# Prefix sums of 14 routing batches as 64-row matmuls around the swap of the row groups

## The chip, the cores and the metric

The kernel runs on one core of one Trainium2 chip. The metric is the device time of one execution in microseconds (us). Engines are named as in the profile: PE (TensorE matmuls), PEld (TensorE weight loads), DVE (VectorE), ACT (ScalarE), POOL (GpSimd), SP (SyncE, which here only issues DMAs).

## The reference

Two parts follow one another: a gated attention unit without softmax, and a mixture of experts with one expert per token beside a dense branch.

```python
# attention: u, v (8, 2816, 256), z (8, 2816, 64)
scores = (1 / S) * (z @ z.T)                 # per batch element
out = np.maximum(scores, 0) ** 2 @ v
x = (u * out).reshape(22528, 256)
# mixture of experts: 8 experts, D 256, F 512
y_dense = relu(x @ w1_dense) @ w2_dense
logits = x @ w_gate
e = argmax(logits); gate = softmax(logits)[e]
y = y_dense + gate * (relu(x @ w1[e]) @ w2[e])
```

For the second part tokens are sorted by expert. Each token's place among the tokens of its expert is a prefix sum over tokens of the one-hot choice, and that sum is what the change touches.

## The kernel before, in words

**Two stages.** Tokens are handled in blocks of 128 (176 blocks, 22 for each of the 8 batch elements). In the attention stage scores, squares and products with `v` are computed, and, block by block, each token's expert and place, after which its row is scattered into the DRAM buffer `xs`, sorted by expert. In the expert stage (`slot`) tiles of sorted rows are fetched, run through the dense branch and one expert, and scattered to the output. The change lies in the attention stage.

**The attention stage.** `scores` (L391) multiplies 64-row pieces of `zT` (the depth of z is 64). `zT` holds z twice, in partitions 0 to 63 and 64 to 127, so that two matmuls run beside each other, one in each half of TensorE's rows (a *row group*), each with its own PSUM bank. `relu` (L413) lets ACT or DVE scale and clamp the result into `r`, and ACT, DVE or at the beginning POOL square it into a key tile `A`. `av` (L578) multiplies two blocks of `A` with `v` into one PSUM pair `o`: 88 matmuls of 64 rows and 256 columns, in two passes. In the first pass row group 0 writes bank 0 and row group 1 bank 1; in the second they change banks (`j = p ^ h`). Each bank collects the sum over both halves of the rows in this way, with no addition afterwards.

**The swap.** Between the passes stands `swap_rows` (L556). It sets something between the last writes of the one row group and the first writes of the other into the same bank: a `touch` (L549, a 64-row matmul of 8 columns into a spare PSUM pair `x`) and two score steps, the first into a pair of its own and the second into `x`; where there are no scores to do, a second touch takes their place.

**PSUM.** There are four pairs of banks (`NS = 4`). `take_pair` and `give_pair` hand them out; `o`, scores, touches, logits and prefix sums all live in one. `keep` holds pairs back near the end of a pass, so that the swap and the next `av` call find one.

**Order of the work.** Engine queues run in program order, and the program order comes from a planner inside the kernel. It carries a planned time `now`, planned times at which ACT, DVE and POOL are free, a list `todo` of offered operations with ready times and ranks, and planned release times of the PSUM pairs. `run(t)` issues what is due until `t`. `fill` (L508), called after every second step of `av`, either starts a due entry of `jobs` when a pair is free, or a score step. `tick` runs after every half `av` call, starts what is listed in `later`, and offers one scatter.

**Routing.** Blocks are routed in 18 batches (`sizes`: 14 of 11 blocks, then 8, 6, 4, 4). `routing(q)` (L1089) puts `first` on `jobs`: it takes a pair, computes `logits` (L652, 2 full-row matmuls of 8 columns for each block) and offers `route_a`, which turns them into the one-hot matrix `oh` (tokens in partitions, experts x blocks along the row). `middle` returns the pair and puts `second` on `jobs`, due 2.5 planned us later. `second` takes a pair, calls `route_pre` (L686) and chains the three DVE steps of `route_b` (L696) behind it. `route_pre` computes, per expert and block, the number of tokens (`ones` times `oh`) and minus the tokens at or after each token (`ntri` times `oh`) into `pre`. `route_b` adds the running base and reads out the places. `last` returns the pair and puts the batch's blocks on the list of `waiting` scatters.

**Scatters and the ring of rows.** `gate_x` (L627), one DVE operation per `av` call, multiplies `o` with `u` into `pays`, a ring of 22 blocks. A scatter (`scatter`, L743: a DVE cast `pi` and a POOL indirect DMA) must have read a block of `pays` before the gate of 22 blocks later overwrites it. Loads of `v`, `z` and the weights are issued by POOL into the same software queue as the scatters.

Of the kernel before, what the change touches and what calls it, by code (L numbers as in the profile page):

```python
# [15 lines left out]
P = 128  # L16
# [3 lines left out]
def kernel(  # L20
# [12 lines left out]
    nc = tc.nc  # L33
    B, S, D = u.shape
    dq = z.shape[2]
    E = moe_w_gate.shape[1]
# [5 lines left out]
    G = 11  # L42
# [3 lines left out]
    nQ = len(sizes)  # L46
# [37 lines left out]
    def banks(x, name, shape=(P, 2, 4 * P), dt=F32):  # L84

        return ps.tile(list(shape), dt, name=name, tag=f"b{x}")
# [7 lines left out]
    ones = const.tile([P, P], BF, name="ones")  # L94
    ntri = const.tile([P, P], BF, name="ntri")
# [39 lines left out]
    now = [0.0]  # L135
# [5 lines left out]
    z_of, zn_of, zT_of, v_of, ut_of, xT_of, lg_of, rs = {}, {}, {}, {}, {}, {}, {}, {}  # L141
# [145 lines left out]
    pairs = [(0.0, x) for x in range(NS - 2)]  # L287
# [42 lines left out]
    def run(until):  # L330
        while True:
            pick = best()
            if pick is None or pick[0][0] > until:
                return
            give(pick)

    def until(cond):

        while cond() is None:
            pick = best()  # L340
            assert pick is not None
            now[0] = max(now[0], pick[0][0])
            give(pick)
        now[0] = max(now[0], cond())
        run(now[0])
# [14 lines left out]
    left, far, key_at = {}, {}, {}  # L360
# [23 lines left out]
    def take_pair():  # L384
        return pairs.pop(0)[1]

    def give_pair(t, x):
        pairs.append((t, x))
        pairs.sort()
# [116 lines left out]
    jobs = []  # L506
# [13 lines left out]
    def ahead(n):  # L520

        for m in range(n, min(n + 3, len(groups))):
            if left[m]:
                if m == n + 2 and (turning and turning[0][0] <= m - 3 or read_at.get(m - 3, 0.0) > now[0]):
                    return None
                return m if groups[m][0] in z_there else None
# [22 lines left out]
    def touch(x):  # L549

        d = banks(x, "d", (P, 8))
        nc.tensor.matmul(out=d[:], lhsT=ones[0:dq, :], rhs=ones[0:dq, 0:8],
                         start=True, stop=True)
        pe(0.03)

    def swap_rows(n):  # L556

        keep[0] = 0
        if ahead(n) is None:
            until(lambda: pairs[0][0] if pairs else None)  # L560
            x = take_pair()
            touch(x)
            touch(x)
            give_pair(now[0] + 0.1, x)
            return
        until(lambda: pairs[1][0] if len(pairs) > 1 else None)
        x = take_pair()
        touch(x)
        m = ahead(n)
        scores(m, left[m].pop(0))  # L570
        m = ahead(n)
        if m is None:
            touch(x)
            give_pair(now[0] + 0.1, x)
        else:
            scores(m, left[m].pop(0), x)
# [67 lines left out]
    bank_of = {}  # L644

    def small(q, name, shape):
        if q < nQ - 2:
            return banks(bank_of[q], name, shape)
        tag = "y" if q == nQ - 2 else "s"
        return late[tag].tile(list(shape), F32, name=name, tag=tag)  # L650
# [34 lines left out]

    def route_pre(q):  # L686
        oh, ex = rs[q]
        pre = small(q, "pre", (P, 2, E * G))
        pre = [pre[:, i, :E * sizes[q]].rearrange("p (e t) -> p e t", e=E) for i in range(2)]
        nc.tensor.matmul(out=pre[0], lhsT=ones[:], rhs=oh, start=True, stop=True)  # L690
        nc.tensor.matmul(out=pre[1], lhsT=ntri[:], rhs=oh, start=True, stop=True)
        rs[q] = (oh, ex, pre)

    first_of = [0]

    def route_b(q):  # L696

        n = sizes[q]
        oh, ex, pre = rs[q]
        inc = vec("inc", E, n)  # L700

        def one():
            se = vec("se", n)
            nc.vector.tensor_reduce(out=se, in_=ex, axis=AX.X, op=ALU.add)
            o = starts[q] % (2 * G)
            rows = pays[:, o:o + n, :]
            nc.vector.reciprocal(rows.bitcast(F32)[:, :, P], se)
            nc.vector.tensor_copy(rows.bitcast(I32)[:, :, P + 1], tok[:, starts[q]:starts[q + 1]])
            assert q != Q1 or made_first[0]
            if first_of[0] != n:  # L710

                first_of[0] = n
                nc.vector.memset(smask[:, :E * n], 1.0)
                nc.vector.memset(smask[:, :E * n].rearrange("p (e t) -> p e t", e=E)[:, :, 0], 0.0)

        def two():
            tb = vec("tb", E, n)
            nc.vector.tensor_copy(tb, pre[0])
            nc.vector.tensor_add(tb[:, :, 0], tb[:, :, 0], base[:])
            nc.vector.tensor_tensor_scan(  # L720
                out=inc.rearrange("p e t -> p (e t)"), data0=smask[:, :E * n],
                data1=tb.rearrange("p e t -> p (e t)"),
                initial=0.0, op0=ALU.mult, op1=ALU.add)
            nc.vector.tensor_copy(base[:], inc[:, :, n - 1])

        def three():
            nc.vector.tensor_add(inc, inc, pre[1])
            nc.vector.tensor_mul(inc, inc, oh)
            pos = vec("pos", n, bufs=5)
            nc.vector.tensor_reduce(out=pos, in_=inc.rearrange("p e t -> p t e"),  # L730
                                    axis=AX.X, op=ALU.add)
            rs[q] = pos

        return [one, two, three]
# [312 lines left out]
    for b in range(B):  # L1047
        t = b * nK
# [30 lines left out]
    def chain(t, fns, then):  # L1079

        def done(t):
            if fns[1:]:
                chain(t, fns[1:], then)
            else:
                then(t)

        offer(t, 0.5, {"dve": (0.8, lambda eng: fns[0]())}, done)

    def routing(q):  # L1089
        def first():  # L1090
            bank_of[q] = take_pair()
            logits(q)
            now[0] += 0.6
            offer(now[0] + 0.2, 0, {"dve": (1.3, lambda eng: route_a(q))}, middle)

        def middle(t):
            give_pair(t, bank_of[q])
            jobs.append((t + 2.5, second))

        def second():  # L1100
            bank_of[q] = take_pair()
            route_pre(q)
            now[0] += 0.25
            chain(now[0] + 0.2, route_b(q), last)

        def last(t):
            give_pair(t, bank_of[q])
            routed.append(q)
            waiting.extend(range(starts[q], starts[q + 1]))

        jobs.append((now[0], first))
# [12 lines left out]
    for q in range(nQ - 2):  # L1124
        t = starts[q + 1] - 1 + LAG
# [26 lines left out]
    for n, (b, i0, w) in enumerate(groups):  # L1152
        for i in range(i0, i0 + w, 2):
# [3 lines left out]
            av(n, i, lambda: tick(g))  # L1157
            tick(g + 1)
    run(9e9)
    while jobs:  # L1160
        jobs.pop(0)[1]()
        run(9e9)
# [3 lines left out]
    for s in range(NT - MAYBE + 2):  # L1166
# [4 lines left out]
        if s % 3 == 1 and waiting:  # L1171
# [5 lines left out]
    n = nc.values_load(used[0:1, 0:1], min_val=0, max_val=NH,  # L1177
                       skip_runtime_bounds_check_because="made by the table")
# [34 lines left out]
```

## Time and profile before

| | |
|---|---|
| median of 3 runs | 913.24 us (909.78 to 918.02) |
| profiled execution | 911.23 us, span 909.5 us, granted clock 0.998 |
| PE busy | 866.3 us, 95% of the span, 12194 matmuls |
| ACT, DVE, POOL busy | 701.5 us (77%), 667.9 us (73%), 475.8 us (52%) |
| o matmuls in the attention stage | 459.9 us busy, 7184 from `A` and 560 from `wall` |
| full-row prefix matmuls | 18 + 18, from 70.2 to 568.0 us |
| DMA | mean 150 GB/s |

A row of a timeline gives the start and the time from the first start to the last end of a merged run of instructions, then line, operation, output<-input, shape and count; in brackets stands the idle time before it and what ended that. A shape `64*128 64x256` is a weight tile of 64 rows and 128 columns and a moving operand of 64 rows and 256 columns. Matmuls overlap, so the spacing of starts counts, not the duration of one.

### The profile page before, as it was taken

The page shows a single profiled execution, that of the slowest core. Times are in us where ns is not written, and L with a number is a line of the kernel's source. Part 1 is how long each engine was busy: PE and PEld are TensorE (multiplying, and loading weights), DVE is VectorE, ACT ScalarE, POOL GpSimd, SP SyncE. Part 2 cuts the span into 40 slices and gives each one's busy share as a digit, 9 for nine tenths or more (in the row PEclk, how much of TensorE's full clock was granted, in tenths as well). Part 3 has the DMA queues.
Part 4 walks back from the last instruction along what each step waited for, and adds up shares of the span by engine and source line. Part 5 has one row for each costly group of instructions (what it writes and reads, how often), then busy time and mean ns, then how long its engine had stood idle before and what let it go on. Part 6 is the DMA issues. An engine that isn't in the chain of part 4 may idle for free. (4 is left out here: it accounts for less than half of the span.)

```text
span 909.5 us, 30158 instructions
## 1 busy us (share of the span) xinstructions
PE 866.3 (95%) x12194; PEld 757.0 (83%) x12194; DVE 667.9 (73%) x1277; ACT 701.5 (77%) x872; POOL 475.8 (52%) x518
## 2 busy tenths in 40 slices
PE   8999999999999999999999999888989999999996
PEld 5898798898898898898888887777878887888885
DVE  7998897998898898889889975555634444456664
ACT  7988797898898888889879973657767676777664
POOL 8202343343443343353344343777878887877664
PEclk9999999999999999999999999999999999999999
DMA  9999999999999989999989966555444444444433
GB/s 178 156 198 156 183 187 172 206 180 184 201 185 175 207 177 184 202 180 183 207 167 163 158 138 104 116 121 109 113 106 112 113 105 109 112 103 100 96 91 80
DMA packets 289294, 136.80 MB, mean 150 GB/s; under 512 B 258686, under 2 KB 266110, under 8 KB 289152
## 3 DMA queue, kind: packets, MB, share of 16 engines
q1 hardware_dynamic: 263552, 79.40, 52.0%
q0 software_dynamic: 25600, 55.44, 26.1%
q8 instruction: 96, 1.57, 0.7%
q14 instruction: 46, 0.38, 0.1%
HBM read 61.54 MB, written 37.16 MB: 109 GB/s over the span
## 5 line engine op out<-in xcount | busy, mean ns | idle before, releaser
L604 PE MATMUL o<-vb,A 64*128 64x256 bf16 x7184 | 459.9, 269 | 2.5 <-ACT A L434 1.5
L604 PEld LDWEIGHTS <-A 64*128 64x128 bf16 x7184 | 379.9, 94 | 42.7 <-ACT A L434 3.5
L750 POOL DMA_INDIRECT xs<-pays,pi x176 | 189.5, 1076 | 278.3 <-DVE pi L748 228.2
L421 ACT ACTIVATE r<-s 128x1024 f32<-128x1024 f32 (+1 forms) x252 | 248.1, 1011 | 43.3 <-PE s L406 40.4
L965 ACT ACTIVATE ring<-h_ps 128x1024 bf16<-128x1024 f32 x180 | 185.5, 1032 | 89.8 <-PE h_ps L962 46.2
L434 ACT ACTIVATE A<-r 128x1024 bf16<-128x1024 f32 (+1 forms) x238 | 241.9, 1046 | 7.9 <-DMA wall<-A 3.3
L986 DVE SCALAR_TENSOR_TENSOR ring<-yy,me,ring 128x256 f32<-128x256 f32 x180 | 86.5, 482 | 152.4 <-ACT ring L985 83.7
L436 DVE TENSOR_TENSOR A<-r 128x1024 bf16<-128x1024 f32 x151 | 183.1, 1223 | 3.5 <-ACT A L434 1.4
L423 DVE TENSOR_SCALAR r<-s 128x1024 f32<-128x1024 f32 (+1 forms) x145 | 176.1, 1221 | 8.1 <-PE s L406 5.5
L988 POOL DMA_INDIRECT out_dram<-ring,me x140 | 148.9, 1064 | 63.1 <-DVE ring L986 29.4
L970 PEld LDWEIGHTS <-ring 128*128 128x128 bf16 x1440 | 139.9, 98 | 41.2 <-issue 25.5
L406 PE MATMUL s<-zT 64*128 64x512 bf16 (+1 forms) x874 | 146.5, 357 | 4.0 <-DVE pays L631 1.3
L970 PE MATMUL yy<-w2d,ring 128*128 128x256 bf16 x720 | 107.9, 272 | 19.5 <-DVE ring L986 16.6
L970 PE MATMUL yy<-ring 128*128 128x256 bf16 x720 | 108.0, 273 | 0.0
L962 PE MATMUL h_ps<-ring,w1d 128*128 128x256 bf16 x720 | 94.1, 273 | 3.1 <-DVE pays L631 1.6
L962 PE MATMUL h_ps<-ring 128*128 128x256 bf16 (+1 forms) x880 | 94.8, 253 | 0.9 <-issue 0.7
L985 ACT COPY ring<-yy 128x256 f32<-128x256 f32 x180 | 68.0, 378 | 34.0 <-PE yy L970 17.2
L950 DVE COPY ring<-wall 128x2048 bf16 x110 | 82.0, 761 | 12.7 <-issue 7.0
L631 DVE TENSOR_TENSOR pays<-o,ut 128x512 bf16<-128x512 f32 x88 | 60.4, 686 | 32.4 <-PE o L604 19.9
L962 PEld LDWEIGHTS <-ring 128*128 128x128 bf16 x880 | 73.4, 98 | 10.6 <-issue 1.9
L962 PEld LDWEIGHTS <-w1d 128*128 128x128 bf16 x720 | 70.0, 98 | 12.0 <-issue 3.5
L406 PEld LDWEIGHTS <-zT 64*128 64x128 bf16 x874 | 55.1, 94 | 21.3 <-issue 9.6
(122 smaller groups left out, 437.1 us busy)
## 6 DMA issues: line engine op xcount, KB each, us to landing
ut<-in_u_dram SPq DMA_DIRECT2D x88, 256.0 KB
vb<-in_v_dram POOLq DMA_DIRECT2D x14, 704.0 KB
wall<-in_moe_w_dram POOLq DMA_DIRECT2D x16, 256.0 KB
xs<-pays,pi POOLq DMA_INDIRECT x176
zr<-in_z_dram POOLq DMA_DIRECT2D x7, 352.0 KB
out_dram<-ring,me POOLq DMA_INDIRECT x140
ring<-xs SPq DMA_TRANSPOSE x114
xT<-pays SPq DMA_TRANSPOSE x88
```

What stands on the lines that cost most here:

```text
L406: nc.tensor.matmul(out=s[:, h, y * c:(y + 1) * c], lhsT=zT[r, k + h, :], rhs=zT[r, i0:i0 + w, :], start=True, stop=True)
L421: nc.scalar.activation(r[:, :, :c], s[:, :, :c], AF.Relu, scale=1.0 / S)
L423: nc.vector.tensor_scalar(out=r[:, :, :c], in0=s[:, :, :c], scalar1=1.0 / S, scalar2=0.0, op0=ALU.mult, op1=ALU.max)
L434: nc.scalar.activation(a, r, AF.Square)
L436: (nc.gpsimd if eng == "pool" else nc.vector).tensor_mul(a, r, r)
L604: nc.tensor.matmul(out=o[:, j, 0:D], lhsT=block(n, k, i + j - i0)[r], rhs=v_of[b][r, k, :], start=(p == 0 and x == 0), stop=(p == 1 and x ...
L750: ins = nc.gpsimd.indirect_dma_start(out=xs, out_offset=bass.IndirectOffsetOnAxis(ap=pi[:], axis=0), in_=pays[:, g % (2 * G), 0:ROW].bitca ...
L962: nc.tensor.matmul(out=h_ps[:, f, hs, :], lhsT=w1(c, f), rhs=xT[:, hs, c, :], start=(c == 0), stop=(c == 1))
L965: nc.scalar.activation(h, h_ps[:].rearrange("p f h t -> p f (h t)"), AF.Relu)
L970: nc.tensor.matmul(out=y[:, k, :], lhsT=h[:, f, j * P:(j + 1) * P], rhs=w2(f), start=(f == 0), stop=(f == 3))
L986: nc.vector.scalar_tensor_tensor(out=ys, in0=y[:, 1, :], scalar=me[:, j, 0:1], in1=yd, op0=ALU.mult, op1=ALU.add)
L988: ins = nc.gpsimd.indirect_dma_start(out=out, out_offset=bass.IndirectOffsetOnAxis(ap=ids[j], axis=0), in_=ys, in_offset=None, bounds_chec ...
```

## The change

For the first 14 routing batches `second` no longer goes to `jobs` but to a list of its own, `at_swap`. The next `swap_rows` that finds an entry due takes it. It runs the prefix matmuls as 64-row pieces: two before the touch (row group 0 with `ones` into bank 0, row group 1 with `ntri` into bank 1), and two after it (row group 0 with `ntri` into bank 1, row group 1 with `ones` into bank 0), which add up with the first two in the two banks. Between them stand the touch and one score step into the touched pair (or a second touch); a usual swap has two score steps there. The last four batches keep the full-row form.

```diff
+    at_swap = []
+
     def swap_rows(n):
 
         keep[0] = 0
+        if at_swap and at_swap[0][0] <= now[0]:
+            fn = at_swap.pop(0)[1]
+            until(lambda: pairs[1][0] if len(pairs) > 1 else None)
+            fn(0)
+            x = take_pair()
+            touch(x)
+            m = ahead(n)
+            if m is None:
+                touch(x)
+                give_pair(now[0] + 0.1, x)
+            else:
+                scores(m, left[m].pop(0), x)
+            fn(1)
+            return
...
     def route_pre(q):
         oh, ex = rs[q]
-        pre = small(q, "pre", (P, 2, E * G))
+        pre = banks(bank_of[q], "pre") if q < nQ - 4 else small(q, "pre", (P, 2, E * G))
         pre = [pre[:, i, :E * sizes[q]].rearrange("p (e t) -> p e t", e=E) for i in range(2)]
-        nc.tensor.matmul(out=pre[0], lhsT=ones[:], rhs=oh, start=True, stop=True)
-        nc.tensor.matmul(out=pre[1], lhsT=ntri[:], rhs=oh, start=True, stop=True)
         rs[q] = (oh, ex, pre)
+        if q < nQ - 4:
+            pre_part(q, 0)
+        else:
+            nc.tensor.matmul(out=pre[0], lhsT=ones[:], rhs=oh, start=True, stop=True)
+            nc.tensor.matmul(out=pre[1], lhsT=ntri[:], rhs=oh, start=True, stop=True)
+
+    def pre_part(q, p):
+
+        oh, _, pre = rs[q]
+        for h in range(2):
+            r = slice(h * dq, (h + 1) * dq)
+            j = p ^ h
+            nc.tensor.matmul(out=pre[j], lhsT=(ones, ntri)[j][r, :], rhs=oh[r],
+                             start=(p == 0), stop=(p == 1))
+        now[0] += 0.04
...
         def middle(t):
             give_pair(t, bank_of[q])
-            jobs.append((t + 2.5, second))
-
-        def second():
-            bank_of[q] = take_pair()
-            route_pre(q)
-            now[0] += 0.25
-            chain(now[0] + 0.2, route_b(q), last)
+            if q < nQ - 4:
+                at_swap.append((t + 2.5, second))
+            else:
+                jobs.append((t + 2.5, lambda: second(0)))
+
+        def second(p):
+            if p == 0:
+                bank_of[q] = take_pair()
+                route_pre(q)
+            else:
+                pre_part(q, 1)
+            if p == 1 or q >= nQ - 4:
+                now[0] += 0.1
+                chain(now[0] + 0.2, route_b(q), last)
```

More of the change, by code (lines that the diff above doesn't have):

```diff
@@ L1159 @@
     run(9e9)
+    assert not at_swap
     while jobs:
```

## The prediction

> **What bounds the kernel now.** I read the summary page first, then the table of stretches, then PE's waits, then PE's timeline around one routing step.
>
> ```profile
> span 909.5 us, 30158 instructions
> PE 866.3 (95%) x12194; PEld 757.0 (83%) x12194; DVE 667.9 (73%) x1277; ACT 701.5 (77%) x872; POOL 475.8 (52%) x518
> ...
> q0 software_dynamic: 25600, 55.44, 26.1%
> ```
>
> The profiled execution took 911.23 us, 1.7 us more than its span. The three runs shown have a median of 913.24, 2.0 us above the profiled one, and lie between 909.78 and 918.02. A measurement of this kernel can hardly tell less than 1% (9.1 us) from no change.
>
> ```profile
> 180.00:240.00 60.00, 59.29 (x1015) 52.24 (x1011) 51.96 (x91) 50.34 (x56) 24.56 (x25) 1.00 1.08 184
> ...
> 300.00:360.00 60.00, 59.57 (x1026) 52.67 (x1022) 52.72 (x99) 51.69 (x57) 24.52 (x25) 1.00 1.02 189
> ...
> 570.00:640.00 70.00, 61.77 (x548) 53.04 (x547) 37.10 (x85) 44.38 (x70) 52.32 (x62) 1.00 0.55 118
> ```
>
> The columns are busy time of PE, PEld, DVE, ACT and POOL, then granted clock, DMA share and GB/s. The attention stage, in which all 14 edited places lie, is PE's: 59.3 to 59.6 us of 60. DVE (52) and ACT (50 to 52) run at some 87%, so each has about 0.8 us of slack in an `av` call (6.1 us, below). DMA is full (1.0 to 1.1). The expert stage behind it is untouched.
>
> ```profile
> PE d L552 <- ACT r L421: 1.4, 1, 1.4
> PE s L406 <- DVE pays L631: 1.3, 3, 0.5
> PE s L406 <- ACT r L421: 0.8, 3, 0.3
> PE s L406 <- DVE r L423: 0.5, 3, 0.2
> PE s L406 <- issue: 0.2, 1, 0.2
> ```
>
> These are all of PE's waits between 60 and 540 us: 4.2 us together. So the attention stage is set by PE's stream itself; an edit pays there through PE time, or hurts through a new wait.
>
> **What the old prefix step costs.** PE's timeline around the first one:
>
> ```profile
> 67.68 0.42 PE L552 MATMUL d<-ones 64*128 64x8 bf16 x2
> 67.95 0.39 PE L604 MATMUL o<-vb,wall 64*128 64x256 bf16 x4
> 68.18 2.13 PE L604 MATMUL o<-vb,A 64*128 64x256 bf16 x36
> 70.24 0.21 PE L690 MATMUL pre<-oh,ones 128*128 128x88 bf16 x1
> 70.28 0.21 PE L691 MATMUL pre<-oh,ntri 128*128 128x88 bf16 x1
> 70.42 0.39 PE L604 MATMUL o<-vb,A 64*128 64x256 bf16 x4
> 70.65 0.38 PE L604 MATMUL o<-vb,wall 64*128 64x256 bf16 x4
> 70.87 0.38 PE L406 MATMUL s<-zT 64*128 64x512 bf16 x2
> 71.08 0.60 PE L604 MATMUL o<-vb,wall 64*128 64x256 bf16 x8
> ...
> 73.27 0.17 PE L552 MATMUL d<-ones 64*128 64x8 bf16 x1
> 73.27 0.65 PE L406 MATMUL s<-zT 64*128 64x512 bf16 x4
> 73.74 0.39 PE L604 MATMUL o<-vb,wall 64*128 64x256 bf16 x4
> ```
>
> The shapes say it: the stream around is 64-row matmuls, of which two run side by side (a pair of o's in (70.65 - 70.42)/2 = 0.11 us, a pair of scores in 71.08 - 70.87 = 0.21 us). The 36 o's from 68.18 are 18 pairs of 0.109, so the stream would go on at 70.15; it goes on at 70.42. The step costs 0.27 us, though its second matmul follows the first by 0.04: most of it is a gap before and after the two full-row matmuls, not their columns. Read in the same way, the 14 places give 0.27 to 0.30.
>
> ```profile
> 510.37 0.40 PE L604 MATMUL o<-vb,A 64*128 64x256 bf16 x4
> 510.70 0.21 PE L690 MATMUL pre<-oh,ones 128*128 128x88 bf16 x1
> ...
> 510.89 1.38 PE L604 MATMUL o<-vb,A 64*128 64x256 bf16 x22
> ```
>
> The last: 510.37 + 2 x 0.11 = 510.59, and on at 510.89: 0.30. **Removed: 14 x 0.28 = 3.9 us.**
>
> **What the new step costs.** In the changed kernel's instruction order each of the 14 places is: two 64-row matmuls into `pre`, one touch, one score pair, two 64-row matmuls into `pre`. All 14 have this form; touches (104), scores (874) and o's (7744) keep their number, so the second score pair that this swap had goes elsewhere at the same price.
>
> - The two pairs of 88 columns. No row shows a 64-row matmul of 88 columns. Below: by columns, 88/256 of an o pair, 0.04. Above: a whole o pair, 0.11, which holds two loads of the same 128 columns. The 22 logits matmuls with as many loads, further down, take 0.64 us, 0.03 each, so two loads need about 0.06. I take 0.05 a pair, 0.10 a place (bounds 0.08 to 0.22).
>
> ```profile
> 134.17 0.62 PEld L660 LDWEIGHTS <-xT 128*128 128x128 bf16 x22 [0.21 <-issue]
> 134.17 0.70 PE L660 MATMUL lg<-wg,xT 128*128 128x8 bf16 x22
> 134.81 2.36 PE L604 MATMUL o<-vb,A 64*128 64x256 bf16 x40
> ```
>
> [...]
>
> - The touch. Before, a swap was a touch, a score pair into another PSUM pair, and a score pair into the touched one: 73.27 to 73.74, 0.47, of which 0.43 are the two score pairs; 0.04 is the swap's own. In the new order the only score pair goes into the touched pair right behind the touch, and its first matmul waits on PE itself, because it is a new tile in the buffer just written. The twin is at 67.68: there the second touch is such a tile, and the stream goes on at 67.95, 0.27 later. So the score starts about 0.26 after the touch, and nothing stands between to hide it. The new swap: 0.10 + 0.26 + 0.21 = 0.57, less its score pair 0.36. Without the wait it would be 0.12.
>
> **Sum on PE:** per place +0.36 - 0.04 - 0.28 = +0.04, 14 x = **+0.5 us** (without the touch's wait -2.8; with the wait and pairs of 0.11, +2.2). Removing the full-row gap is nearly paid back by the wait that the shorter swap lays bare.
>
> **What moves.** The step no longer starts at the first free place 2.5 us after the first routing half, but at the next swap: 24 or 48 o's later, 1.3 or 2.6 us, in all but the fourteenth place, where it comes 4 o's earlier. Behind it come twelve small DVE instructions, which keep their cover (DVE's slack), and behind these the scatters of the batch, a DVE `pi` and a POOL DMA each half `av` call.
>
> - PSUM: `pre` holds one of four pairs until its last reader. Before, in every second batch it held one while a score wanted it; that is what the three waits on `pays` show (140.00 `pre`, 141.59 the score):
>
> ```profile
> 140.00 0.21 PE L690 MATMUL pre<-oh,ones 128*128 128x88 bf16 x1
> ...
> 141.59 0.39 PE L406 MATMUL s<-zT 64*128 64x512 bf16 x2 [0.53 <-DVE pays L631]
> ```
>
> In the new order the scores at these places come while `pre` holds nothing. I take the 1.3 us as gone, and the other waits as they are (bounds: all 4.2 gone; a wait of 0.5, the longest of this kind, at all 14 swaps: +7). The one of 1.4 is the first pair's release at a swap, and this swap is now one with `pre` in it; I leave it.
>
> - Scatters and the gate. The DVE gate (L631) overwrites a row pair of `pays` that a scatter must have read. In DVE's old order three or four scatters beyond the needed one stand before a gate, in the new one two or three. Before, between 90 and 520 us, the needed scatter's issue ended 8.3 to 14 us ahead of the gate, mostly about 10.4. The shortest of these (328.52 to 336.83, 8.3), and a shorter one at the end:
>
> ```profile
> L631 DVE TENSOR_TENSOR pays<-o,ut x88: 674/684/759, 19.8 to 554.9; 128x512 bf16<-128x512 f32 x88
> ...
> 326.82 1.70 POOL L750 DMA_INDIRECT xs<-pays,pi  x1 [3.09 <-DVE pi L748]
> ...
> 336.83 0.69 DVE L631 TENSOR_TENSOR pays<-o,ut 128x512 bf16<-128x512 f32 x1
> ...
> 542.50 1.00 POOL L750 DMA_INDIRECT xs<-pays,pi  x1 [0.30 <-issue]
> ...
> 548.83 0.69 DVE L631 TENSOR_TENSOR pays<-o,ut 128x512 bf16<-128x512 f32 x1 [0.39 <-PE o L604]
> ```
>
> A gate comes every (554.9 - 19.8)/87 = 6.15 us and two scatters with it, so one scatter less is 3.1 us and leaves some 7.3 of 10.4. The last lead was 543.50 to 548.83, 5.3 us, and what ended that gate's wait was PE. DMA was less loaded there, but 7.3 is well above it. Cost zero; the cover's loss is the slower rival.
>
> - Queues. SP's order differs only in that a few block transposes of `A` stand two to five entries later in three batches; POOL's in that scatters and weight loads exchange places. PE waits for no DMA in the list above. Zero. ACT gets four squarings more and three relus less, DVE the reverse:
>
> ```profile
> L434 ACT ACTIVATE A<-r 128x1024 bf16<-128x1024 f32 (+1 forms) x238 | 241.9, 1046 | 7.9 <-DMA wall<-A 3.3
> L436 DVE TENSOR_TENSOR A<-r 128x1024 bf16<-128x1024 f32 x151 | 183.1, 1223 | 3.5 <-ACT A L434 1.4
> ```
>
> About 1 us to and fro on engines with 13% slack.
>
> Together 911.2 + 0.5 - 1.3 = 910.4 for a profiled execution, and with the 2.0 us by which the runs' median lies above, **912.4 us**: no change that can be told.
>
> **Rivals.** (1) The touch's wait is hidden: if the score's wait on PE is as free as in the old swaps, the sum is -2.8, and with all of PE's 4.2 us of waits gone 911.2 - 7.0 = 904.2, 906.2 as a median; faster, not by 1%. For it: the old swaps carry this wait at no cost. Against: there a pair of 0.21 us stood between, here nothing. More than 9.1 us is not to be had from PE's gaps in this stage. (2) The step doesn't do what it says: the small pairs don't overlap with the stream, and each costs a gap as the full-row step did, 0.28: 14 x (0.56 - 0.10) = +6.4, and 912.4 becomes 918.8. Against: touches of the same height (73.27) pass without a gap. (3) Slower: scatters that stand behind a load of v in the software queue land later than the new lead. A v half is 704 KB; at the queue's row (55.44 MB in 26.1% of 909.5 us, 4.3 ns a KB) it takes 3.0 us of all engines, and at half of them about 6, so a scatter behind it lands some 7 us after its issue. From 7.3 on the gate waits, and everything behind it on DVE, the relus that PE's scores need. With two loads a batch and 2 us each, beyond 0.8 of slack: 14 x 1.2 = 17 us, and 912.4 becomes 929.4. For it: the lead shrinks in every batch. Against: no gate waits for a scatter now, even at 5.3.
>
> **How the numbers follow.** Forecast 0.56, rival 1 0.19, rival 2 0.07, rival 3 0.13; 0.05 for a gain above 1% by a schedule that meets fewer waits in the expert stage too. Within 1% is 0.56 + 0.19 + 0.07 = 0.82, slower 0.13, faster 0.05. The forecast's own range: 912.4 - 3.3 and + 1.7 for PE's bounds, more for the spread of the runs (-3.5, +4.8). The range goes from 906 (rival 1) to 921 (rival 2 and half of the upper spread) and leaves rival 3 out.
>
> **What would show it.** Right: at each swap with `pre`, PE's timeline has about 0.26 us between touch and score and 0.57 from the first `pre` to the next o; no full-row `pre` inside the o stream before 515 us; no `PE s <- DVE pays` at the seconds. Wrong: a touch directly followed by the score (rival 1), small `pre` pairs of 0.2 us or more (rival 2), or DVE `pays` idle with a releaser long done and PE waits on `pays` growing (rival 3). The attention stage moving by more than 5 us would refute the sum.

## The result, and the profile after

The changed kernel is slightly slower. On the chip of the first comparison the median of 18 runs was 919.22 us (912.57 to 926.15) against 912.99 us (905.38 to 989.22) for 18 runs of the kernel before. The ratios in this document, each with a 95% interval, are taken over the runs within 1.5% of the fastest of their kernel: here 1.0088 [1.0059, 1.0116], where the two medians give 1.0068. Two later comparisons gave 1.0049 [1.0016, 1.0082], on a chip where the kernel before took 912.29, and 1.0049 [1.0013, 1.0084], on one where it took 876.65. So it is slower by 0.5 to 0.9% (0.4 to 0.7% by the medians): inside the 1% that one measurement can tell, outside no change. Kernels on different chips are compared by ratios alone.

The profiled execution took 926.03 us, so it is one of the slowest of the 18, and what it shows is not the usual run. Its page, and two stretches of it (columns as before: PE, PEld, DVE, ACT, POOL busy, granted clock, DMA share, GB/s):

```profile
span 924.3 us, 30213 instructions
PE 869.5 (94%) x12222; PEld 763.4 (83%) x12222; DVE 667.7 (72%) x1276; ACT 701.4 (76%) x873; POOL 491.1 (53%) x518
```

```profile
180.00:240.00 60.00, 55.98 (x936) 49.32 (x932) 49.54 (x83) 49.37 (x54) 24.29 (x24) 0.97 1.11 164
300.00:360.00 60.00, 59.12 (x1025) 53.07 (x1023) 52.64 (x100) 50.82 (x57) 24.37 (x23) 1.00 1.07 193
```

In one stretch PE is nearly as full as it was (59.1 of 60 us, 59.6 before), in the other 3.3 us are missing and the granted clock has a dent, 0.97. The logits matmuls mark the end of the attention stage. Their groups (min/median/max ns, first to last start) of the kernel before, of the changed one, and of the changed one in the second comparison:

```profile
L660 PE MATMUL lg<-wg,xT x352: 166/166/180, 64.9 to 564.0; 128*128 128x8 bf16 x176
```

```profile
L676 PE MATMUL lg<-wg,xT x352: 166/166/181, 64.7 to 575.3; 128*128 128x8 bf16 x176
```

```profile
L676 PE MATMUL lg<-wg,xT x352: 166/166/180, 64.4 to 565.6; 128*128 128x8 bf16 x176
```

Of the 14.8 us between the two spans (924.3 and 909.5) 11.3 arise ahead of the last logits. But the second profile of the same program (span 914.6) comes to its last logits only 1.6 us later than the kernel before, so the 11.3 are lost in single events, not in every swap. In both profiles 3.5 us more pass behind the last logits than before (349.0 against 345.5), in the expert stage; in the second these are most of its 5.1. No experiment below looks at them. They may not be the change's: on other chips that part took 314.8 and 314.0 us in the old order (the ring of 24 and the two scatters of the experiments) and 313.9 in the changed kernel. The longer waits of PE between 60 and 540 us in the first profile:

```profile
PE d L552 <- ACT r L421: 4.0, 2, 2.2
PE d L552 <- DVE wall L261: 3.1, 1, 3.1
PE s L406 <- DVE pays L647: 2.8, 6, 0.7
```

With 0.7 us of shorter ones these are 10.6 us, where the kernel before had 4.2. The three waits of a score for `pays` have become six.

**The swap with the prefix sum in it**, PE's timeline of the changed kernel:

```profile
144.37 0.40 PE L620 MATMUL o<-vb,A 64*128 64x256 bf16 x4
144.59 0.20 PE L719 MATMUL pre<-oh,ones 64*128 64x88 bf16 x1
144.60 0.20 PE L719 MATMUL pre<-oh,ntri 64*128 64x88 bf16 x1
144.62 0.17 PE L552 MATMUL d<-ones 64*128 64x8 bf16 x1
144.90 0.39 PE L406 MATMUL s<-zT 64*128 64x512 bf16 x2
145.11 0.20 PE L719 MATMUL pre<-oh,ntri 64*128 64x88 bf16 x1
145.13 0.20 PE L719 MATMUL pre<-oh,ones 64*128 64x88 bf16 x1
145.15 0.40 PE L620 MATMUL o<-vb,wall 64*128 64x256 bf16 x4
```

From the first `pre` to the next o 0.56 us, of which 0.28 lie bare between touch and score, and a pair of `pre` takes 0.03 to 0.04.

**The largest event.** POOL, DVE and PE in the timeline of the changed kernel, with the piece of the chain of waits (start, us, what) that joins them:

```profile
205.47 0.57 POOL L131 DMA_DIRECT2D vb<-in_v_dram  x1 [0.65 <-DVE pi L777]
206.35 0.98 POOL L779 DMA_INDIRECT xs<-pays,pi  x1 [0.30 <-issue]
...
220.86 0.69 DVE L647 TENSOR_TENSOR pays<-o,ut 128x512 bf16<-128x512 f32 x1 [4.98 <-DMA xs<-pays,pi]
...
221.61 0.16 PE L552 MATMUL d<-ones 64*128 64x8 bf16 x1 [3.14 <-DVE wall L261]
```

```profile
206.35 14.32 DMA xs<-pays,pi
220.86 0.69 DVE pays L647
...
241.04 6.92 DMA wall<-A
```

A scatter is issued 0.9 us behind a half load of v and lands after 14.3 us. The gate waits 4.98 us for it, PE's touch 3.14 us for what stands behind the gate on DVE. The logits of the batch before this came 1.3 us later than in the kernel before (202.65 against 201.36), the next ones 6.7 us later (241.21 against 234.54). The second large event, at 241 to 250, is a block transpose of `A` that holds ACT and, through it, the touch of a swap with `pre` in it:

```profile
248.12 1.06 ACT L434 ACTIVATE A<-r 128x1024 bf16<-128x1024 f32 x1 [3.41 <-DMA wall<-A]
...
250.14 0.16 PE L552 MATMUL d<-ones 64*128 64x8 bf16 x1 [2.21 <-ACT r L421]
```

After both pauses, and after one of 1.78 us at 106.05, PE ran for a while at half clock, 0.50 (PE, PEld, DVE, ACT, POOL, clock, DMA, GB/s):

```profile
106.00:108.00 2.00, 1.89 (x19) 1.35 (x20) 1.90 (x7) 2.00 (x4) 0.40 (x1) 0.65 1.18 203
108.00:110.00 2.00, 2.00 (x22) 1.77 (x20) 1.47 (x6) 2.00 (x3) 0.57 (x1) 0.50 1.05 231
...
223.00:225.00 2.00, 2.00 (x22) 1.42 (x20) 2.00 (x3) 1.83 (x2) 2.00 (x3) 0.50 0.97 228
...
250.00:252.00 2.00, 1.80 (x15) 1.12 (x16) 1.84 (x6) 2.00 (x4) 0.32 (x1) 0.50 1.18 204
```

### The profile page after: what moved, and what is told of

Same layout as the page of the kernel before. It is cut to its first block, busy times and chain, and to the rows that moved or that the text cites. A ratio compares the mean times of both kernels' runs of the same rounds, so it can differ in the third digit from the quotient of the medians.

```text
span 924.3 us, 30213 instructions
## 1 busy us (share of the span) xinstructions
PE 869.5 (94%) x12222; PEld 763.4 (83%) x12222; DVE 667.7 (72%) x1276; ACT 701.4 (76%) x873; POOL 491.1 (53%) x518
## 4 chain that ended last, share of the span: by engine, by line
PE 67%; POOL 9%; issue 9%; DVE 5%; DMA 4%; ACT 3%; POOLq 1%; SPq 0%; DVEq 0%; ACTq 0%
PE o L620 39%; PE h_ps L991 9%; PE yy L999 9%; PE s L406 9%; POOL out_dram L1017 7%; DMA xs<-pays,pi 2%; DMA wall<-A 1%; PE lg L676 1%; DVE ring L1015 1%; DVE r L423 1%; DMA vb<-in_v_dram 1%; DVE pays L647 1%; ACT A L434 1%; POOL zr L1004 1%; DVE A L436 1%
## 5 line engine op out<-in xcount | busy, mean ns | idle before, releaser
L620 PEld LDWEIGHTS <-A 64*128 64x128 bf16 x7184 | 384.1, 94 | 45.4 <-issue 5.4
L779 POOL DMA_INDIRECT xs<-pays,pi x176 | 205.5, 1168 | 284.3 <-DVE pi L777 158.5
L434 ACT ACTIVATE A<-r 128x1024 bf16<-128x1024 f32 (+1 forms) x242 | 245.9, 1043 | 9.7 <-DMA wall<-A 7.9
L436 DVE TENSOR_TENSOR A<-r 128x1024 bf16<-128x1024 f32 x147 | 177.6, 1222 | 8.2 <-ACT r L421 7.2
L423 DVE TENSOR_SCALAR r<-s 128x1024 f32<-128x1024 f32 (+1 forms) x148 | 179.0, 1221 | 5.4 <-POOL A L436 1.8
L1014 ACT COPY ring<-yy 128x256 f32<-128x256 f32 x180 | 68.2, 379 | 25.7 <-PE yy L999 14.5
L991 PEld LDWEIGHTS <-ring 128*128 128x128 bf16 x880 | 73.8, 98 | 11.7 <-DVE ring L979 2.4
```

Source lines behind the costliest of these rows:

```text
L423: nc.vector.tensor_scalar(out=r[:, :, :c], in0=s[:, :, :c], scalar1=1.0 / S, scalar2=0.0, op0=ALU.mult, op1=ALU.max)
L434: nc.scalar.activation(a, r, AF.Square)
L436: (nc.gpsimd if eng == "pool" else nc.vector).tensor_mul(a, r, r)
L620: nc.tensor.matmul(out=o[:, j, 0:D], lhsT=block(n, k, i + j - i0)[r], rhs=v_of[b][r, k, :], start=(p == 0 and x == 0), stop=(p == 1 and x ...
L779: ins = nc.gpsimd.indirect_dma_start(out=xs, out_offset=bass.IndirectOffsetOnAxis(ap=pi[:], axis=0), in_=pays[:, g % (2 * G), 0:ROW].bitca ...
L991: nc.tensor.matmul(out=h_ps[:, f, hs, :], lhsT=w1(c, f), rhs=xT[:, hs, c, :], start=(c == 0), stop=(c == 1))
```

## The experiments

**The theories.** One: the loss lies in the new swap itself, in its 64-row matmuls and the bare wait behind the touch (the swap theory). The other: it comes from the step's later time: the scatters of the batch start later, the *lead* of the scatter that a gate needs gets shorter, and gates catch scatters that land late, above all behind a load of v (the lead theory). A third, called the pair theory in the expectations: `pre` holds one of the four PSUM pairs through the swap, so the touch has to wait for ACT to give another one free. (PE theory there is the swap theory without this, theory load is the lead theory.) The lead is counted along the timelines of POOL and DVE: gate n (from 0) overwrites rows that scatter 2n-21 has to have read (2n-23 with a ring of 24); below it runs from the start of that scatter on POOL to the start of the gate, as a mean over the gates between 137 and 500 us.

| kernel | ratio to before | mean lead, us | needed scatter is the one right behind a v load (us to its gate) | gate waits for a scatter, us (times) |
|---|---|---|---|---|
| before | 1 | 11.7 | none | none |
| changed | 1.0088, 1.0049, 1.0049 | 8.9, 8.5, 8.4 | both loads of a batch element (7.5 to 10.0; once 14.5) | 5.3 (2), 0.6 (1), 0.2 (1) |
| old form, all routing one tick later | 1.0120 | 8.8 | both (8.9 to 11.5) | 2.7 (1) |
| full-row form at the swap | 1.0042 | 8.7 | both (8.1 to 9.6; once 13.3) | 4.0 (1) |
| at the swap, even batches only | 1.0018 | 8.7 | the second (8.8 to 9.1; once 13.1); behind the first it is issued 2.3 us after the load (7.7; once 9.8) | 7.7 (2) |
| at the swap, odd batches only | 0.9939 | 11.2 | none | none |
| the same in full rows | 0.9959 | 11.2 | none | none |
| changed, ring of 24 | 1.0018 | 14.4 | both (14.1 to 14.6) | none |
| before, ring of 24 | 1.0006 | 17.7 | none | none |
| changed, two scatters a tick | 1.0055 | 12.8 | both (14.1 to 14.5) | none |
| changed, logits a tick earlier | 1.0287 | 12.8 | none | 3.9 (3) |
| 64-row form in mid-pass | none on record | 14.0 | two of the loads (12.3) | 23.9 (4) |

(Gate waits from 60 to 560 us of the one profile that each run has.)

When a scatter landed can be read from the last update of its semaphore on record (some updates are missing, so it may have landed later). Between 80 and 500 us the twelve scatters right behind a load of v took 5.9 to 9.5 us in the changed kernel and once 14.3, all others a median of 4.4. In the kernel before the twelve took 5.9 to 8.8 and once 11.6, and no gate needed them. In the changed kernel with the ring of 24 one of them took 13.1 us, and its gate still found it done 1.5 us earlier. So such landings come in both orders; the order decides whether a gate meets them.

**1. Time or form.** Four kernels on one chip: the changed one again; the old full-row form with all routing one tick later; the changed one with logits one tick earlier and the step due 1.5 us earlier; and the step at the swap, but in full rows.

```diff
 # b_lag6: the kernel before with
+        t = starts[q + 1] - 1 + LAG + (1 if q < Q1 - 1 else 0)
 # a_early: the changed kernel with LAG 4 instead of 5 and
-                at_swap.append((t + 2.5, second))
+                at_swap.append((t + 1.0, second))
 # a_full_row25: the changed kernel, both full-row matmuls in fn(0), none in fn(1)
+        nc.tensor.matmul(out=pre[0], lhsT=ones[:], rhs=oh, start=True, stop=True)
+        nc.tensor.matmul(out=pre[1], lhsT=ntri[:], rhs=oh, start=True, stop=True)
```

> The changed kernel once more, for a second profile and for the comparisons of this group. It measured 919.2 us against 913.0 (ratio 1.0088). Its first profile lost 5.4 us at one place (a gate that waited 5.0 us for a scatter issued behind a load of v, then half clock) and 3.4 at another (ACT waiting for a block transpose). Lead theory: such events come in nearly every execution, at varying places, 6 us in all. PE theory (the touch's wait and the small matmuls cost 0.4 us a place): no such event needed, the 14 swaps themselves are 0.4 us longer each. Pair theory: waits of the touch at the swaps with pre. All: 917 to 921.

> The kernel before with routing started one tick (half an av call) later for the first 13 batches: full-row matmuls where they were, but two or three scatters beyond the needed one ahead of each gate, as in the changed kernel, instead of three or four. Lead theory: about 919, with waits of gates on scatters or of PE behind them. PE theory and pair theory: 913, no change.

> The changed kernel with routing started one tick earlier and its second half due 1.0 planned us after the first, so that 7 of 14 prefix steps fall on the swap before and the lead is three to four scatters again. The 64-row matmuls at the swap stay. Lead theory: 911 to 914. PE theory and pair theory: 919, as the changed kernel.

> The changed kernel with the two full-row matmuls set at the swap, ahead of the touch, and nothing behind it: the same order on all engines but for the form of these matmuls. Lead theory and pair theory: 919 to 922 (the full-row gap comes on top). PE theory: the small matmuls were the cost, so 913 to 915.

Measured: 1.0049 [1.0016, 1.0082], 1.0120 [1.0068, 1.0172], 1.0287 [1.0241, 1.0334] and 1.0042 [1.0007, 1.0077]. The old form, only later, loses at least as much as the change; the step at the swap in full rows loses about the same as in 64 rows. So the change's loss does not need the 64-row form. PE's timeline of the full-row step at the swap:

```profile
140.90 0.40 PE L620 MATMUL o<-vb,A 64*128 64x256 bf16 x4
141.23 0.21 PE L707 MATMUL pre<-oh,ones 128*128 128x88 bf16 x1
...
141.86 0.40 PE L620 MATMUL o<-vb,wall 64*128 64x256 bf16 x4
```

141.12 (140.90 + 2 x 0.11) to 141.86 is 0.74, 0.18 more than 0.56, or 2.5 us over 14 places: too little to be told apart in these totals. In both kernels that are late without the 64-row form a gate met a late scatter, in the later old form at 345.53, again right behind a load of v:

```profile
334.89 0.60 POOL L131 DMA_DIRECT2D vb<-in_v_dram  x1
335.79 1.02 POOL L750 DMA_INDIRECT xs<-pays,pi  x1 [0.30 <-issue]
...
345.53 0.69 DVE L631 TENSOR_TENSOR pays<-o,ut 128x512 bf16<-128x512 f32 x1 [2.67 <-DMA xs<-pays,pi]
```

But this kernel's gates waited longer for other things, two of them for a block transpose, so its 1.2% are not the late scatter's alone:

```profile
DVE pays L631 <- DMA wall<-A: 8.1, 2, 4.1
```

The kernel with earlier logits was a miss: it got its lead (12.8 us), and yet gates waited 3.9 us for scatters, and PE stood 16.0 us in seven waits that no semaphore explains, so its time says nothing about the lead.

```profile
PE o L620 <- issue: 16.0, 7, 4.5
```

The DMA packets in its trace point to a reason: each of the six longest of these waits ends 1.3 to 1.6 us after a 16 KB packet of the instruction queue (`q8 instruction` on the page) has ended, though such packets come only every 8.3 us in the mean. PE seems to have waited for its next instructions; no run tests it.

**2. More scatters, smaller loads of v, the new form in the old place.** On another chip (the repeat of the quarters on the chip of the third group):

```diff
 # a_two (changed), b_two (before): in tick, behind one_scatter()
+            if len(waiting) > 8:
+                one_scatter()
 # a_v4, a_v4_2 (changed): v in quarters instead of halves
+            for h in range(4):
+                soon(t + (11, 13, 15, 17)[h], lambda b=b, h=h: load_v(b + 1, h, 4))
 # b_row64 (changed, but from jobs as before): the 64-row pieces in mid-pass
-                at_swap.append((t + 2.5, second))
+                jobs.append((t + 2.5, lambda: second_here()))
+        def second_here():
...
+            second(0)
...
+            touch(x)
+            if m is not None:
+                scores(m, left[m].pop(0), x)
...
+            second(1)
```

> The changed kernel with one more scatter per tick while more than eight blocks of a batch wait, so that the scatters of a batch run some three blocks earlier against the gates and ahead of the load of v. The prefix steps stay at the swaps. Lead theory (a gate catches a scatter that queued behind a load of v): no such wait, 911 to 914. PE theory (the swaps themselves) and pair theory: 916 to 919, as the changed kernel.

> Control: the kernel before with the same extra scatter per tick. All theories: 911 to 914, no change, since its gates wait for no scatter; if it becomes faster or slower, the other run with two scatters must be read against it.

> The changed kernel with v loaded in four quarters (ticks 11, 13, 15, 17 of a batch element) instead of two halves (13, 15): 352 KB instead of 704 ahead of a scatter. Lead as in the changed kernel. Lead theory: a scatter waits behind half as much, 913 to 916. If the late scatter has nothing to do with v: 916 to 919.

> The four 64-row matmuls with a touch and a score step between them, but started from jobs as in the kernel before, in mid-pass and without waiting for a swap; lead three to four scatters. Lead theory: 911 to 914 with PE's own sum near zero (0.10 + 0.24 against 0.28 a place, +0.8). If the 64-row form is the cost, 916 to 919.

> The changed kernel with v in quarters, again, beside the changed kernel on the same chip. Theory load: ratio 1.000 to 1.004 and below the changed kernel's. Theory swap: the changed kernel's ratio.

Measured: 1.0055 [1.0026, 1.0085], 0.9997 [0.9955, 1.0040], 1.0020 [0.9985, 1.0054] and, repeated, 1.0041 [1.0008, 1.0074] for the quarters. With a second scatter the changed kernel had 14.1 us and more at the v loads and no gate waited for a scatter, yet it won nothing: a miss for the lead theory, and the time that the others expected. Its waits moved to the other side, squarings that wait for block transposes (`ACT A <- DMA wall<-A`, 14.0 us in six) and touches behind them:

```profile
PE d L552 <- ACT r L421: 8.9, 5, 2.6
```

So the lead is not the only way to lose here. All five of these touches stand at swaps with `pre` in them, as do the touches at 106.05 and 250.14 of the changed kernel's first profile and the only one that waits for ACT in its second (1.73 us) and third (0.44), though only 14 of some 90 touches do; in the kernel before with the same two scatters no touch waited over 0.3 us. That is what the pair theory says. Against it stand the touch at 106.50 in the kernel before, which waited 1.41 us with no `pre` about, and the odd batches below. No run keeps `pre` from holding a pair at the swap, so this rival stays open. With v in quarters no gate named a scatter in one profile and one did for 0.8 us in the other; the totals do not separate it from the changed kernel.

The new form in mid-pass, with a long lead, took 926.78 us (six runs, 909.9 to 934.6) where the kernel before took 876.86 (29 runs, up to 897.15); no ratio is on record. The four matmuls cannot be that loss, at 0.03 to 0.04 us a pair, nor did this kernel lack lead (14.0 us in the mean). In its profile (924.91 us, granted clock 0.978) PE, gates and scatters wait in turn; a scatter issued at 146.64 took 20.75 us.

```profile
DVE pays L650 <- DMA xs<-pays,pi: 23.9, 4, 8.7
```

Both theories expected at most 919 us on the scale of the first chip, so both missed. What starts these phases stays open. They show that landing times themselves are no constant.

**3. Without loads of v.** Both kernels with the loads of v for the batch elements 1 to 7 left out, the changed kernel beside them:

```diff
 # in load_v
+        if b > 0:
+            v_of[b] = v_of[0]
+            free["pool"] = max(free["pool"], now[0]) + 0.8
+            return
```

> The changed kernel a third time, as the common measure of this group (absolute times differ between chips; the ratio to the kernel before is what counts). Both theories: ratio 1.004 to 1.010.

> The changed kernel without the same 14 loads; order of all other instructions, the prefix steps at the swaps and the lead of two to three scatters as in the changed kernel. Theory load (scatters queued behind a load of v land late, and the shorter lead makes the gate catch them): same time as the kernel before without the loads, at most 2 us more for the swaps. Theory swap (the 14 swaps with prefix steps cost by themselves, or by pairs): still 4 to 7 us slower than the kernel before without the loads.

> The kernel before without the 14 loads of v behind the first batch element (the first element's v is used for all, so the output is not the reference's). Control for the next run. Both theories: a ratio within 0.995 to 1.002, as none of its gates waits behind a load.

Measured against the kernel before: 1.0049 [1.0013, 1.0084] for the changed kernel, 1.0092 [1.0060, 1.0124] and 1.0071 [1.0041, 1.0102] without v. The control missed its 0.995 to 1.002: without the loads both are slower, as the output differs and with it the routing (from the last logits on they took 322.9 and 324.0 us, the changed kernel with its loads 313.9). So only the difference counts: 0.0021, against 0.0049 with v, with overlapping intervals. The totals decide nothing. The profiles do say something. Without v, with the short lead, no gate waited for a scatter, and the two are level up to their seventeenth logits step, at 550.75 us with the change and 550.87 without, so the swaps themselves cost nothing that shows. (The last logits come 4.0 us later with the change; there PE waits 2.5 us for rows of the expert stage.) In the changed kernel beside them, in the chain of waits, the scatter right behind a load sets a gate and through it a score:

```profile
329.01 0.40 POOL vb L131
...
329.90 7.57 DMA xs<-pays,pi
...
338.01 0.70 DVE pays L647
...
338.76 0.39 PE s L406 x2
```

This gate stood 3.94 us, the same gate without the loads 3.28 to 3.30 in every round, for the last o. The cost is small: this execution was the fastest of its twelve (873.34 us, median 880.73) and came to its seventeenth logits step at 551.12.

**4. The lead by itself, and half the batches.** A ring of 24 blocks gives each row one more `av` call. Besides, the pool `rt` goes from two buffers to one, and batches that wrap around the ring need two small DVE instructions more:

```diff
 # a_ring24 (changed), b_ring24 (before)
-    rt = pool("rt", 2)
+    rt = pool("rt", 1)
...
+    RING = 2 * G + 2
+    pays = const.tile([P, RING, WIDE], BF, name="pays")
 # a_even, a_odd: at_swap only for q < nQ - 4 and q % 2 == 0 (or 1), the others as before
```

> The changed kernel with a ring of 24 blocks for the rows (pays) instead of 22, so that four to five scatters beyond the needed one stand ahead of each gate; order of all engines as in the changed kernel, but for two small DVE instructions more in batches that wrap around the ring. Lead theory: ratio 0.998 to 1.003. Swap theory: 1.005 to 1.009, unchanged.

> Control: the kernel before with the same ring of 24 blocks (five to six scatters beyond the needed one). Both theories: 0.998 to 1.002, since its gates already find their scatters done.

> Only the seven even batches have their prefix step at the swap (48 o matmuls later than before), the odd ones in full rows in mid-pass as before. Lead two to three scatters for most gates. Lead theory: 1.004 to 1.009. Swap theory: 1.000 to 1.002, since the waits of the touch came at swaps of odd batches.

> Only the seven odd batches have their prefix step at the swap (24 o matmuls later than before), the even ones in full rows in mid-pass as before. Lead three scatters for nearly all gates. Lead theory: 1.000 to 1.003. Swap theory: 1.004 to 1.009.

Measured: 1.0018 [0.9993, 1.0042], 1.0006 [0.9975, 1.0038], 1.0018 [0.9992, 1.0044], 0.9939 [0.9915, 0.9962]. With the long lead the change costs 0.0012 between the two rings, which is nothing that can be told; this is what the lead theory expected. The two halves went against it: the even batches alone gave the swap theory's 1.000 to 1.002, and the odd ones alone came out faster than either theory allowed. What PE does without events is seen from one logits step to the one two batches on, first in the changed kernel with the long ring, then in the old one with it:

```profile
268.37 0.71 PE L677 MATMUL lg<-wg,xT 128*128 128x8 bf16 x22
...
334.81 0.70 PE L677 MATMUL lg<-wg,xT 128*128 128x8 bf16 x22
```

```profile
266.63 0.70 PE L661 MATMUL lg<-wg,xT 128*128 128x8 bf16 x22
...
333.03 0.70 PE L661 MATMUL lg<-wg,xT 128*128 128x8 bf16 x22
```

66.44 against 66.40: +0.02 us a place.

With only the even batches at the swap gates were late behind a load of v, but the kernel lost less than the 1.004 to 1.009 of the lead theory:

```profile
337.11 0.58 POOL L131 DMA_DIRECT2D vb<-in_v_dram  x1 [0.74 <-DVE pi L780]
337.99 0.98 POOL L782 DMA_INDIRECT xs<-pays,pi  x1 [0.30 <-issue]
...
342.18 0.69 DVE L650 TENSOR_TENSOR pays<-o,ut 128x512 bf16<-128x512 f32 x1 [5.36 <-DMA xs<-pays,pi]
...
351.05 0.69 DVE L650 TENSOR_TENSOR pays<-o,ut 128x512 bf16<-128x512 f32 x1 [2.34 <-DMA xs<-pays,pi]
```

The first of these two gates needed a scatter issued at 332.35, between the two loads, the second the one right behind the second load.

With only the odd ones the lead stays at 11.2 us, the scatters right behind the loads are not the ones that the next gates wait for, and the kernel is faster than the other two. From 134.46 us on its batches follow one another at 32.74 and 33.66 us in turn (within 0.01) until 466 us; PE waits three times between 60 and 540 us:

```profile
PE d L552 <- ACT r L421: 2.2, 1, 2.2
PE s L406 <- ACT r L421: 0.4, 1, 0.4
PE o L623 <- issue: 0.3, 1, 0.3
```

**5. What the gain of the odd batches hangs on.** The same with the full-row form at the swap, and with the ring of 24:

> Only the odd batches at the swap, lead three scatters, with the two full-row matmuls set ahead of the touch: the order of all engines as in the run with the odd batches at the swap, but for the form of these matmuls. Theory order (the time comes from where the routing step stands): 0.992 to 0.998 as there. Theory form (the 64-row matmuls save PE time): 0.998 to 1.003.

> Only the odd batches at the swap, in 64-row matmuls, with the ring of 24 blocks (lead five scatters). Lead theory: as fast as with 22 blocks or a little faster, 0.990 to 0.996, since a lead of three is mostly enough. If leads of three still meet late scatters: below 0.992.

Measured: 0.9959 [0.9932, 0.9986] and 0.9930 [0.9903, 0.9958]. The three intervals overlap. The gain is there without the 64-row form and without still more lead, so what is left is the order; that the order makes it is argued, not shown. The last has the lowest ratio of this study, 874.39 us where the kernel before took 878.9. Which waits of the kernel before it avoids stays open: a clean round of two batches takes 66.40 us in the old order too (with the ring of 24, above), as it does here (267.26 to 333.66 with the odd batches), so the gain must lie in the old order's events, and no profile of that kernel from this chip was taken.

Taking the touch's wait away was not tried; what the sums in a bank would be without it is not shown.

## Why the prediction was wrong

**Right: what the swap costs.** Forecast 0.57 us for the new swap, 0.26 between touch and score, 0.05 for a pair; measured 0.56, 0.28 and 0.03 to 0.04 (0.55 or 0.56 at 13 of the 14 places with the ring of 24). The sum of +0.04 a place was +0.02 in undisturbed rounds. That the small pairs overlap (against rival 2) and that the touch's wait is bare (against rival 1) held; the swap theory fell with it. The measured 919.22 lies inside the forecast's 906 to 921, but that is luck: the range reached so far up for rival 2, which did not happen.

**Wrong: "I take the 1.3 us as gone".** The waits of scores on `pays` grew from three to six, 1.3 to 2.8 us. They stand at the places where no `pre` is in the way any more:

```profile
352.69 0.69 DVE L647 TENSOR_TENSOR pays<-o,ut 128x512 bf16<-128x512 f32 x1 [4.01 <-PE s L406]
...
353.43 0.39 PE L406 MATMUL s<-zT 64*128 64x512 bf16 x2 [0.43 <-DVE pays L647]
```

So the PSUM pair held by `pre` was not their reason. All six follow a gate that starts some 0.7 us late (a wait of 4.0 to 4.2 instead of 3.2 to 3.3) and whose scatter stands right behind a load of v, 8.1 to 8.3 us ahead. The scatter does not look like the reason on this chip: its last update on record came 0.7 to 2.4 us ahead of these gates (0.2 us ahead of the gate at 220.86), the chain of waits names a score on PE, and the three late gates of the kernel before had a scatter 12.5 to 12.8 us ahead. Only on the other chip does the chain name the scatter (338.01, above). What makes these gates late stays open. The term is +1.5 where the sum had -1.3.

**Wrong: the touch's 1.4 us, "I leave it".** In the first profile the touches at swaps with `pre` waited 4.0 us in two, in the second 1.7 in one. What `pre` has to do with it is the open rival of the second group above.

**Wrong, and the step that the traces refute best: "Cost zero" for scatters and the gate.** The size of the lead was right: 7.3 us forecast from the end of an issue, 8.4 to 8.9 measured from its start, of which the issue is about 1. What failed is the cover. The reason given against rival 3, that a lead of 5.3 us was harmless, came from the end of the stage, where no load of v stands in the queue and the DMA share was 0.78 (540 to 550 us; 1.02 and 1.08 in the two stretches within the stage). Within the stage the shorter lead makes the scatter behind each load the very one that the next gate needs; before, no needed scatter stood there. Rival 3's mechanism is thus the one that the traces show: four kernels have a profile with a gate waiting 2.3 to 5.0 us for just such a scatter (4.98 in the changed one), and with a longer ring, or without the loads, none does. Its estimate of some 7 us to landing was close to the common case (7.6) and far from the rare one (14.3). Its price, 1.2 us at each of 14 loads or 17 us, was too high: in the changed kernel's three profiles a gate waited for a scatter once for 4.98 us and else for under 1 us; the whole loss was 0.5 to 0.9%. How much of that loss the late scatters are is not shown: the second profile has only 0.6 us of such waits, two scatters a tick took them away and the time stayed, and the ring's 1.0018 beside 1.0049 to 1.0088 has intervals that touch in two of three comparisons, on different chips. The gates in the table and the landing times are the stronger evidence that the mechanism is there.

**Not foreseen: what a pause costs beyond itself.** The 3.14 us at 221.61 delayed the logits by 5.4. Part of the rest is the half clock behind it: 0.50 from 222.64 to 226.05 us, which holds back some 1.7 us of PE's work, an estimate from these two times. Pauses of 1.78 and 2.21 us were followed by 0.50 too. Length alone does not decide: with two scatters a tick a pause of 2.19 us at 173.67 was followed by 0.50 and one of 2.64 us at 244.56 by 1.00. The kernel before had one of 1.41 at the same place as the first and kept a clock of 1.00:

```profile
106.00:108.00 2.00, 1.50 (x25) 1.17 (x26) 1.84 (x5) 2.00 (x3) 0.97 (x1) 1.00 1.14 212
```

**The transposes** (event at 250) were counted as free, since PE waited for no DMA before. The change moves few of them, and which part of their lateness is the change's is not shown.

## What to carry to other kernels

When a step moves, ask of each transfer behind it not only how much lead is left on average but which transfer now is the last one that a consumer needs, and what stands ahead of that one in its queue; a harmless short lead in a quiet stage (5.3 us here) proves nothing for a busy one. A cover of 8.4 to 8.9 us, beside landings mostly of 5.9 to 9.5, cost the gates 5.3, 0.6 and 0.2 us in three profiles here, so look at several profiles of the same program before calling such a cover free or dear. And move a step only in those rounds where its consumers can bear it: here the seven odd moves alone made the kernel faster and all fourteen made it slower.

## What the runs showed of the hardware

- A scatter on the software queue right behind a half load of v (704 KB) landed 5.9 to 9.5 us after its issue and once 14.3 in the changed kernel's first profile, other scatters a median of 4.4 (between 80 and 500 us); in the kernel with the 64-row form in mid-pass one took 20.75 us.
- Two 64-row matmuls of 88 columns in different row groups cost 0.03 to 0.04 us in a stream of 64-row matmuls (144.59 to 144.62 and 145.11 to 145.15 in the changed kernel); two full-row ones cost 0.27 to 0.30 in the kernel before, though they start only 0.04 apart (70.24 and 70.28). From a touch to the score pair right behind it in the same PSUM pair 0.28 us passed (144.62 to 144.90).
- Half clock (0.50) followed PE pauses of 1.78, 2.21 and 3.14 us in the changed kernel's first profile and one of 2.19 with two scatters a tick (at 173.67); pauses of 1.41 (kernel before, at 106.50), 2.16 (odd batches, at 106.64) and 2.64 us (two scatters a tick, at 244.56) left the clock at 1.00.
- The six longest of PE's seven waits without a semaphore in the kernel with earlier logits (16.0 us in all, the longest 4.5) ended 1.3 to 1.6 us after a 16 KB packet of the instruction queue.
- Two chips differed by 4% for the changed kernel (medians 915.57 and 880.73), most of it in the expert stage: 914.6 - 565.6 = 349.0 us from the last logits to the end of the span on the one, 871.6 - 557.7 = 313.9 on the other.
